# Values of both attentions as one product by seven block products, in a float32 gated mix of two attentions

## The chip, the cores and the metric

The kernel runs on one core of a Trainium2 chip. The metric is the device time of one execution in microseconds (us), the median of several. A core has TensorE (PE, with its weight loads PEld), VectorE (DVE), ScalarE (ACT), GpSimd (POOL) and SyncE (SP, which here issues nearly all DMAs). Each engine works through its own list of instructions strictly in order; an instruction that waits for another engine or for a DMA holds up all that stand behind it on the same engine.

## The reference, cut to what matters

```python
x = A_x                                       # 1 x 2048 x 512, float32
g = sigmoid((x * gate_w).sum(-1))
# A: 32 heads of 16, softmax over all 2048 keys
q, k, v = split(x @ A_wqkv)
a = softmax(q k^T / 4) v  -> (2048 x 512) @ A_wo
# B: 4 segments of 512 with a causal mask inside a segment and a memory M, z across them
q, k, v = x @ B_wq, x @ B_wk, x @ B_wv
for s in range(4):
    a_dot = softmax(q_s k_s^T / 4 + mask) v_s
    a_mem = (phi(q_s) M) / (phi(q_s) z + 1e-6)
    o_s   = sigmoid(beta) * a_mem + (1 - sigmoid(beta)) * a_dot
    M, z  = M + phi(k_s)^T v_s, z + sum phi(k_s)
b = o @ B_wo
out = g * a + (1 - g) * b
```

So x is multiplied by six 512x512 weights: A's q, k, v and B's q, k, v. This change is about the two v.

## The kernel before, in words

**Precision.** TensorE's fast float32 format (fp32r) keeps fewer bits, so every operand is split into a high part (a cast on ACT) and a low part (a subtraction of the cast from the original, on DVE or POOL), and every product is three matmuls: low by high, high by low, high by high (`PARTS`). One 512x512x512 product thus costs 4 (rows) x 4 (depth) x 3 = 48 matmuls of 128x512.

**Two stages.** The first 280 us prepare: the projections of x (here called X, in four chunks of 512 tokens), their stores to DRAM in the layout that the heads want, B's memory, the gate. The second stage, from the first score (line 1045) on, is the attention proper with scores, exponentials and products with v. The change lies in the first stage alone. 96 row maxima are wanted there ahead of the scores: `some_max` computes four of them at a time, with four matmuls (line 242) and four reductions on DVE (line 275), and `loads(n)` brings the q and k rows that they use back from DRAM.

**Slots.** The first stage is written as a sequence of slots. `slot` issues 12 matmuls of 128x512, in four places of three, and behind each place it calls the functions that were posted for that slot and place: copies out of PSUM, casts, subtractions, stores, loads. A posted function only puts instructions at the ends of the engines' lists; the slot number thus sets the order on every engine, and the semaphores set the time. Before the change there are 86 slots:

- slots 0 to 7: values of A for chunks 0 and 1 (`v_tiles`, four slots each);
- slots 8 to 15: queries of A for chunks 0 and 1 (`qk_tile`, one slot for each 128 rows of the output);
- slots 16 to 22: keys of A for chunks 0 and 1 as one 512x1024 product. `pair_tiles` cuts it in blocks, 2 by 2 in the weights and 2 by 2 in X, and makes it out of seven block products instead of eight, by Winograd's scheme: block sums S of X (`s_sums`, `s_split`) and T of the weights (`t_sum`, `t_split`), seven products in PSUM, and sums of these in `out_tile` and `sums`, on DVE;
- slots 23 to 30 values of A for chunks 2 and 3, slots 31 to 37 their keys in the same seven products;
- slots 38 to 85: for each chunk four slots of B's queries, four of B's values, four of B's keys. Behind B's queries and keys come phi, the products of the memory (`mem_q`, `mem_k`).

The groups of first maxima start in slot s0+12 = 50 and stand in 8 of each 12 slots; `loads(0)` is posted for slot s0+6 = 44. In the code `s0` is 38.

**Engines in the first stage.** ACT makes the copies out of PSUM (line 432, 537) and the casts (433, 479, 575); DVE the low parts of the results (440, 485), most low parts of operands (576), the sums out of PSUM (476, 500, 502); POOL the block sums of the weights (663), those of X for chunks 2 and 3 (646 to 649), some low parts (576), `tensor_scalar_min` for phi (437) and small DMAs, among them eight that spread `beta` over partitions (line 740, slot 8). PSUM has eight banks of 128x512: two of `pr_ps`, two of `me_ps`, four of `me_sm`. A matmul into a bank waits until the bank's last reader is through. SP's DMAs use eight semaphores in turn, so an issue waits for the landing of the eighth before it. Results' high and low parts pass through three buffers each (`q1`, `q2`): a cast into one waits until the store from it three results earlier has landed.

Of the kernel before, what the change touches and what calls it, by code (L numbers as in the profile page):

```python
# [10 lines left out]
F32 = mybir.dt.float32  # L11
# [8 lines left out]
D = 512  # L20
H = 32
DH = 16
CH = 512
# [24 lines left out]
def gated_mix(ctx, tc, x, xT, wqkv, a_wo, b_wq, b_wk, b_wv, b_wo, beta, gate_w, out):  # L48
# [284 lines left out]
    with ExitStack() as p0:  # L333
        wp = p0.enter_context(tc.tile_pool(name="wp", bufs=1))
        raws = p0.enter_context(tc.tile_pool(name="raws", bufs=3))
        xp = p0.enter_context(tc.tile_pool(name="xp", bufs=1))
        vp = p0.enter_context(tc.tile_pool(name="vp", bufs=1))
# [11 lines left out]
        ones = wk1.tile([2, CH], F32, name="ones")  # L349
        nc.vector.memset(ones, 1.0)  # L350

# [8 lines left out]
        def slot(products=()):  # L362

            for place in range(4):
                for ps, l, r, start, stop in products[3 * place:3 * place + 3]:
                    nc.tensor.matmul(ps, l, r, start=start, stop=stop)  # L366
                for f in posted.pop((now[0], place), []):
                    f()
            now[0] += 1
# [8 lines left out]


        def halves(pool, tag, src, load_slot, split_slot, tiles=None, queue=nc.sync, eng=nc.vector):  # L380

            hold = {}

            def load(i):
                t = tiles[i] and tiles[i]() if tiles else None
                if t is None:
                    t = raws.tile([128, 2, D], F32, tag="raw", name="raw")
                if isinstance(t, list):
                    for k in range(2):
                        queue.dma_start(t[k], src[256 * i + 128 * k:256 * i + 128 * k + 128])  # L390
                        hold["raw", 2 * i + k] = t[k]
                else:
                    queue.dma_start(t, src[256 * i:256 * i + 256].rearrange("(k p) d -> p k d", p=128))
                    for k in range(2):
                        hold["raw", 2 * i + k] = t[:, k]

            def split(k):
                if k == 0:
                    hold[0] = pool.tile([128, KT, D], F32R, tag=tag + "h", name=tag + "h")
                    hold[1] = pool.tile([128, KT, D], F32R, tag=tag + "l", name=tag + "l")  # L400
                w = hold["raw", k]
                nc.scalar.copy(hold[0][:, k], w)
                eng.tensor_sub(hold[1][:, k], w, hold[0][:, k].bitcast(F32))
            if load_slot is None:
                load(0)
                load(1)
            else:
                ls = load_slot if isinstance(load_slot, tuple) else (load_slot,) * 2
                post_at(ls[0], 2, lambda: load(0))
                post_at(ls[1], 3, lambda: load(1))  # L410
            for k in range(KT):
                post_at(split_slot + k // 2, 2 * (k % 2), lambda k=k: split(k))
            return hold
# [4 lines left out]
        def qk_tile(w, xc, o, dst, then=None, side="B", bank=None):  # L418

            ps = bank() if bank else pr_ps.tile([128, CH], F32, tag="pr", name="pr")  # L420
            whole(ps, lambda a, k: w[a][:, k, o * 128:(o + 1) * 128], lambda b, k: xc[b][:, k, :])
# [17 lines left out]
            def e1():  # L439
                nc.vector.tensor_sub(q2, full, q1.bitcast(F32))  # L440
# [14 lines left out]
        def pair_tiles(w, ts, xs, ss, cs, dst, eng_):  # L455

            steps, odd = [], [0]
            for g in range(2):
                col = slice(128 * g, 128 * g + 128)

                def quarter(i, j, col=col):
                    return lambda a, k: w[a][:, 2 * i + k, 256 * j:256 * j + 256][:, col]
# [946 lines left out]
```

## Time and profile before

| what | value |
|---|---|
| time, three runs | 1745.16, 1745.83, 1746.33 us (median 1745.83) |
| span of the profiled execution, first to last instruction | 1744.5 us, 1.3 us under the median |
| busy: PE, DVE, ACT, POOL | 1738.4, 1597.1, 1436.5, 736.5 us |
| granted TensorE clock | 1.000 |
| first score matmul (line 1045) | 279.9 us |

The page gives shares of the whole span; the first stage is one sixth of it, so its own busy times are to be read from windows of the trace. Times in the trace are from the span's start. Where a group of instructions has a mean in ns, that is the mean duration of one; a row of the timeline gives start, duration (of all, where several are joined with x2) and, in brackets, how long the engine sat idle before and for whom.

### The profile page before, as it was taken

What the parts mean: (1) busy time and instruction counts of PE and PEld (TensorE: products, weight loads), DVE (VectorE), ACT (ScalarE), POOL (GpSimd) and SP (SyncE); (2) the same over time, 40 slices, a digit from 0 to 9 for tenths busy, and PEclk for the clock granted to TensorE, in tenths of its full rate; (3) what the DMA queues carried; (4) which work ended last, traced back from release to release, by engine and by line L of the source; (5) the groups of instructions that cost most, each with busy time, mean ns of one, the idle gap of its engine ahead of it and who ended that gap; (6) DMA issues with size and microseconds to landing.
All of it is one profiled execution on the core that took longest, in us unless ns stands there. A gap on an engine that the chain in (4) does not pass through costs nothing.

```text
span 1744.5 us, 41555 instructions
## 1 busy us (share of the span) xinstructions
PE 1738.4 (100%) x15205; PEld 885.8 (51%) x15205; DVE 1597.1 (92%) x3327; ACT 1436.5 (82%) x2763; POOL 736.5 (42%) x992
## 2 busy tenths in 40 slices
PE   9999999999999999999999999999999999999999
PEld 7887775444444444444444444444444444444445
DVE  7757788999999999999999999999999999999931
ACT  6545557888888898888888888888888888888884
POOL 3543233234352427352534353535344353535443
PEclk9999999999999999999999999999999999999999
DMA  6787567335453446454545454444445444545542
GB/s 209 251 291 227 194 226 215 110 102 145 127 153 105 138 119 183 131 137 136 143 122 157 122 143 130 134 145 122 149 130 148 130 127 124 148 115 147 149 154 63
DMA packets 149387, 261.62 MB, mean 150 GB/s; under 512 B 39064, under 2 KB 61624, under 8 KB 148672
## 3 DMA queue, kind: packets, MB, share of 16 engines
q1 hardware_dynamic: 146640, 254.42, 49.2%
q0 software_dynamic: 2400, 4.29, 0.9%
q8 instruction: 121, 1.98, 0.5%
q14 instruction: 82, 0.67, 0.1%
q10 hardware_dynamic: 144, 0.26, 0.1%
HBM read 174.39 MB, written 83.25 MB: 148 GB/s over the span
## 4 chain that ended last, share of the span: by engine, by line
PE 99%; ACT 0%; DMA 0%; DVE 0%; issue 0%; SPq 0%; ACTq 0%; DVEq 0%
PE ops L155 40%; PE st L1045 28%; PE sm L242 14%; PE pr L366 9%; PE pair L366 4%; PE sm L155 2%; PE mt_ps L232 0%; PE tps L831 0%; PE sm L1045 0%; DMA vs<-wqkv 0%; PE mps L845 0%; PE num L804 0%; PE den L808 0%; ACT p L1068 0%; DVE pm L275 0%
## 5 line engine op out<-in xcount | busy, mean ns | idle before, releaser
L1068 ACT ACTIVATE p<-st 128x512 f32<-128x512 f32 x2261 | 1190.7, 600 | 147.6 <-PE sm L242 98.6
L275 DVE TENSOR_REDUCE pm<-sm 128x1 f32<-128x512 f32 x2048 | 1276.5, 683 | 9.7 <-PE sm L242 8.7
L242 PE MATMUL sm<-kA,qA 48*128 48x512 f32 x2048 | 662.5, 424 | 0.1
L1045 PE MATMUL st<-qA,kA 50*128 50x512 f32 x2014 | 656.2, 432 | 0.0
L155 PE MATMUL ops<-p,vA 128*17 128x256 f32 (+3 forms) x6360 | 553.0, 445 | 0.0
L1045 PEld LDWEIGHTS st<-qA,kA 50*128 50x128 f32 x2014 | 326.8, 185 | 423.4 <-ACT p L1068 378.9
L242 PEld LDWEIGHTS sm<-kA,qA 48*128 48x128 f32 x2048 | 337.8, 185 | 11.3 <-DVE ph L449 3.9
L1169 POOL TENSOR_TENSOR rcp<-rec,minus 128x32 f32<-128x32 f32 x43 | 234.8, 5461 | 78.3 <-DMA rec<-dend 73.5
L290 DVE CUSTOM_DVE_ANT_0 rest<-sm,mask 128x128 f32<-128x128 f32 (+3 forms) x512 | 246.8, 482 | 0.8 <-PE sm L242 0.7
L155 PEld LDWEIGHTS ops<-p,vA 128*17 128x17 f32 x6360 | 129.2, 96 | 216.1 <-issue 185.0
L1049 POOL TENSOR_SCALAR_AFFINE_SELECT p<-p 128x512 f32<-128x512 f32 x128 | 79.4, 637 | 270.4 <-ACT p L1068 265.7
L242 PE MATMUL sm<-kB,qB 48*128 48x128 f32 (+3 forms) x512 | 166.1, 384 | 0.0
L1045 PE MATMUL st<-qB,kB 50*128 50x512 f32 (+1 forms) x495 | 105.4, 330 | 0.3 <-ACT mt L235 0.3
L1045 PEld LDWEIGHTS st<-qB,kB 50*128 50x128 f32 x495 | 68.6, 186 | 62.2 <-ACT p L1068 50.5
L155 PE MATMUL ops<-p,vB 128*17 128x128 f32 (+3 forms) x1504 | 88.3, 350 | 0.0
L242 PEld LDWEIGHTS sm<-kB,qB 48*128 48x128 f32 x512 | 79.9, 184 | 0.0
L214 POOL TENSOR_TENSOR dm<-pm 128x32 f32<-128x32 f32 x32 | 7.9, 247 | 169.9 <-DVE pm L275 169.9
L437 POOL TENSOR_SCALAR mn<-full 128x512 f32<-128x512 f32 x24 | 36.7, 1527 | 75.6 <-ACT full L432 75.6
L223 POOL CAST ms<-pm 128x16 fp32r<-128x16 f32 x32 | 6.3, 196 | 127.5 <-DVE pm L290 127.5
L1185 POOL TENSOR_TENSOR v<-v,inv 128x512 f32<-128x512 f32 x31 | 39.8, 1283 | 28.1 <-DMA inv<-rdA 21.9
L155 PEld LDWEIGHTS ops<-p,vB 128*17 128x17 f32 x1504 | 33.8, 96 | 30.1 <-issue 26.1
L440 DVE TENSOR_TENSOR q<-full,q 128x512 fp32r<-128x512 f32 x40 | 29.2, 731 | 18.6 <-ACT q L433 15.8
(319 smaller groups left out, 1690.9 us busy)
## 6 DMA issues: line engine op xcount, KB each, us to landing
kA<-kdA SPq DMA_DIRECT2D x256, 128.0 KB
vA<-vdA SPq DMA_DIRECT2D x31, 544.0 KB
kA<-kdA SPq DMA_DIRECT2D x256, 64.0 KB
qB<-qdB SPq DMA_DIRECT2D x192, 64.0 KB
kB<-kdB SPq DMA_DIRECT2D x192, 64.0 KB
kdA<-q SPq DMA_DIRECT2D x32, 256.0 KB
qdB<-q SPq DMA_DIRECT2D x32, 256.0 KB
qA<-qdA SPq DMA_DIRECT2D x64, 128.0 KB
```

What stands on the lines that cost most here:

```text
L155: behind[0] = nc.tensor.matmul(*args, **kw)
L242: nc.tensor.matmul(ps[:, n0:n0 + n], rows(qt[u][:, :, s * 128:(s + 1) * 128], h, 48), rows(k[:, :, k0:k0 + n], h, 48), start=True, stop=True)
L275: nc.vector.tensor_reduce(pm[:, h, s, kc:kc + 1], ps, axis=AX.X, op=ALU.max, negate=True)
L290: nc.vector.tensor_tensor_reduce(out=tri["rest"][:, 0:w], in0=ps[:, n0:n0 + w], in1=tri["mask"][:, CH - w:], scale=-1.0, scalar=3.0e38, op ...
L366: nc.tensor.matmul(ps, l, r, start=start, stop=stop)
L437: nc.gpsimd.tensor_scalar_min(ph["mn"], full, 0.0)
L440: nc.vector.tensor_sub(q2, full, q1.bitcast(F32))
L1045: nc.tensor.matmul(ps[:, n0:n0 + CH - q0], rows(k[:, :, b * 128:(b + 1) * 128], h, 50), rows(q[:, :, q0:], h, 50), start=True, stop=True)
L1049: nc.gpsimd.affine_select(out=x, in_=x, pattern=[[0, 4], [1, 128]], base=0, channel_multiplier=-1, compare_op=ALU.is_ge, fill=0.0)
L1068: nc.scalar.activation(p[:, h], ps, AF.Exp, scale=SCALE)
L1169: eng.tensor_tensor(r, rec, minus, op=ALU.pow)
L1185: eng.tensor_mul(k["v"], k["v"], k["inv"])
```

## The change

**One product for both values.** The weights of A's and B's values stand side by side as one 512x1024 matrix W = (A's wv, B's wv). For a pair of chunks, X (1024 tokens) by W is again a 2 by 2 by 2 block product, and `v_pair` makes it of seven products of block sums instead of eight, for chunks 0, 1 and for chunks 2, 3. A block product of v_pair is two slots (24 matmuls). B's values are thus ready for all chunks ahead of the B slots; they are stored to `vdB` in DRAM and brought back by `load_vB` for the memory products.

**Sums in PSUM.** `k_pair` takes the place of `pair_tiles`. In both the products p1, p6, p5, p3 add into one bank X and p7, p4 add into one bank Y (p2 has Y before them), so that only three sums are left to DVE for an output group instead of seven. In return an accumulating bank must be copied out (ACT) between two products that both add to it.

**Slots now: 82.** v_pair's p1 and p2 are slots 0 to 3; A's queries for chunks 0 and 1 slots 4 to 11 (`fill=queries`); p6, p7, p5, p3, p4 slots 12 to 21; the keys of chunks 0 and 1 slots 22 to 28, those of chunks 2 and 3 slots 29 to 35; values for chunks 2 and 3 in two halves of seven slots, 36 to 42 and 43 to 49; then, for each chunk of B, four slots of queries and four of keys, 50 to 81 (`S0 = 50`). Matmuls of 128x512 at the slots' line go from 1032 to 984.

**First maxima.** One group behind each of the slots 38 to 49, and then behind every second slot of 50 to 81 (three of these places are the memory's). `loads(0)` is posted for slot 36, `loads(16)` for slot 37.

**Moved work.** T3, T4 of the value weights and S3 of X are formed on POOL, the low parts of T1 to T4 too, the key weights' block sums and most of their low parts as well, and the low parts of the key results of p5 and p3. Weights that POOL's queue loaded are loaded by SP. Values that are sums go from DVE straight into the tile `vs` (`tensor_add` with a PSUM input). Tiles are shared otherwise (`unit4`, `pieces`); B's x chunks and weights are brought in by a new `staged`.

Core of the diff, with `...` where it is cut:

```diff
-        def pair_tiles(w, ts, xs, ss, cs, dst, eng_):
...
+        ORDER = (("p1", "11", "11"), ("p2", "12", "21"), ("p6", "S2", "T2"), ("p7", "S3", "T3"), ("p5", "S1", "T1"),
+                 ("p3", "S4", "22"), ("p4", "22", "T4"))
+        def k_pair(xo, cs):
...
+            def done(p, g):
+                if p == "p1":
+                    t["1", g] = copy_x(g, "full")
+                elif p == "p2":
+                    V.tensor_add(t["1", g], Y[g], t["1", g])
+                    out_tile(g, 0, t["1", g], g, V)
+                elif p == "p6":
+                    t["a", g] = copy_x(g, "am")
+                elif p == "p5":
+                    t["5", g] = copy_x(g, "full")
+                    V.tensor_add(t["5", g], Y[g], t["5", g])
+                    out_tile(2 + g, 1, t["5", g], g, P)
+                elif p == "p3":
+                    out_tile(2 + g, 0, copy_x(g, "full"), g, P)
+                elif p == "p4":
+                    V.tensor_add(t["a", g], Y[g], t["a", g])
+                    out_tile(g, 1, t["a", g], g, V)
...
+        def v_pair(xo, cs, bs, fill=None, tags=("full", "full", "am", "am")):
...
+            ybanks = [pr_bank, pr_bank, me_bank, me_bank] if len(bs) == 4 else [me_bank] * 2
+            for p, x, w in ORDER:
+                x, w = xo[x], vops[w]
+                if fill and p == "p6":
+                    fill()
...
+        for n, place, f in ((6, 3, lambda: t_sum("T1", *vb, V)), (7, 0, lambda: t_sum("T3", *vb, P)),
+                            (7, 1, lambda: s_sum("S1", x0, x1, V)), (7, 2, lambda: t_sum("T2", *vb, V)),
+                            (7, 3, lambda: s_sum("S3", x0, x1, P)), (8, 2, lambda: s_sum("S2", x0, x1, V)),
+                            (9, 0, lambda: t_sum("T4", *vb, P)), (9, 1, lambda: op_split(vops["T2"], vr[1][2:4], P)),
...
-        for n in range(5):
-            post_at(s0 + 6 + 3 * n, 2, lambda n=n: loads(16 * n))
-        for n in range(12, 64):
-            if n in (18, 30, 42):
-                post_at(s0 + n, 3, lambda c=n // 12: mem_q(c))
-            elif n // 12 > 2 or n % 12 < 8:
-                post_at(s0 + n, 3, some_max)
+        for n in range(36, S0):
+            if n == 36:
+                post_at(n, 0, lambda: loads(0))
+                post_at(n + 1, 0, lambda: loads(16))
+            elif n > 37:
+                post_at(n, 3, some_max)
+        v_pair(xo1, (2, 3), range(2), tags=("full", "full"))
+        v_pair(xo1, (2, 3), range(2, 4), tags=("full", "full"))
```

**POOL's list ahead of product p6.** Before, from its first memsets on; `ph`, `am` and `raw` hold raw weights or X, the `kB` tiles and `wql` are low parts, `gh` is the gate of the heads:

```order
14 L740 DMA gh<-beta 16x4x1 x8
15 L663 TENSOR_TENSOR ph<-ph 128x256 x2
16 L663 TENSOR_TENSOR ph<-am,ph 128x256 x2
17 L663 TENSOR_TENSOR am<-am,ph 128x256 x2
18 L663 TENSOR_TENSOR am<-am 128x256 x2
19 L576 TENSOR_TENSOR kB_200<-ph,tk 128x256 x2
20 L576 TENSOR_TENSOR kB_201<-ph,tk 128x256 x2
21 L576 TENSOR_TENSOR kB_200<-am,tk 128x256 x2
22 L576 TENSOR_TENSOR kB_201<-am,tk 128x256 x2
```

After the change, same place; the first row is T3's sums, the second S3's, the fourth T4's, and the fifth the low parts of T2, which p6 multiplies:

```order
13 L605 TENSOR_TENSOR u_245<-u_245 128x512 x2
14 L594 TENSOR_TENSOR u_247<-u_246,u_247 128x512 x2
15 L756 DMA gh<-beta 16x4x1 x8
16 L605 TENSOR_TENSOR u_244<-u_244,u_245 128x512 x2
17 L403 TENSOR_TENSOR u_255<-u_245,u_255 128x512 x2
18 L403 TENSOR_TENSOR u_256<-u_245,u_256 128x512 x2
19 L403 TENSOR_TENSOR u_626<-u_244,u_626 128x512 x2
20 L403 TENSOR_TENSOR u_647<-u_244,u_647 128x512 x2
```

The sums are 128x512 instead of 128x256; four of them stand ahead of the eight DMAs, and six more sums and eight DMAs stand ahead of T2's low parts.

**DVE's list at the same time.** After the change, between the first query results and product p6; rows 19, 21, 25, 27, 29 are low parts of query results, row 23 is T1's sums, for which POOL's row 13 waits, and row 26 T2's:

```order
19 L434 TENSOR_TENSOR q_402<-full,q_401 128x512
20 L403 TENSOR_TENSOR u_254<-u_245,u_254 128x512
21 L434 TENSOR_TENSOR q_423<-full,q_422 128x512
22 L403 TENSOR_TENSOR u_254<-u_245,u_254 128x512
23 L605 TENSOR_TENSOR u_244<-u_245,u_244 128x512 x2
24 L594 TENSOR_TENSOR u_247<-u_247 128x512 x2
25 L434 TENSOR_TENSOR q_450<-full,q_449 128x512
26 L605 TENSOR_TENSOR u_245<-u_245,u_244 128x512 x2
27 L434 TENSOR_TENSOR q_487<-full,q_486 128x512
28 L594 TENSOR_TENSOR u_246<-u_247,u_246 128x512 x2
29 L434 TENSOR_TENSOR q_518<-full,q_517 128x512
30 L403 TENSOR_TENSOR u_258<-u_246,u_258 128x512 x2
```

All of these have both inputs in SBUF; the same stretch before holds the sums S of X and the low parts of X and of the key weights instead.

**SP's list at the first loads for the maxima.** Before, the loads of `loads(0)` (line 177) stand behind the stores of B's queries of chunk 0 (line 429):

```order
76 L429 DMA qdB_107<-q_1338 128x512
77 L429 DMA qdB_107<-q_1339 128x512
78 L429 DMA qdB_115<-q_1365 128x512
79 L429 DMA qdB_115<-q_1366 128x512
80 L177 DMA qA_1421<-qdA_59 16x1024
81 L177 DMA qA_1421<-qdA_59 32x1024
82 L177 DMA qA_1421<-qdA_59 16x1024
83 L177 DMA qA_1421<-qdA_59 32x1024
84 L177 DMA kA_192<-kdA_60 32x1024
```

After, they stand directly behind the last stores of the keys of chunks 2 and 3:

```order
62 L465 DMA kdA_66<-q_1194 128x512
63 L465 DMA kdA_66<-q_1195 128x512
64 L465 DMA kdA_74<-q_1205 128x512
65 L177 DMA qA_1220<-qdA_59 16x1024
66 L177 DMA qA_1220<-qdA_59 32x1024
67 L177 DMA qA_1220<-qdA_59 16x1024
68 L177 DMA qA_1220<-qdA_59 32x1024
69 L177 DMA kA_192<-kdA_60 32x1024
```

The maxima that use these rows came six slots behind the loads' place in the program (44 to 50), and now come two slots behind it (36 to the end of 38).

**ACT's list at the keys of chunks 2 and 3.** Before, at their end: casts of finished sums (line 479), each of which waits for DVE, and one copy of a p1 (line 492):

```order
84 L479 CAST q_1142<-full 128x512
85 L479 CAST q_1160<-full 128x512
86 L492 COPY p_1170<-pair 128x512
87 L479 CAST q_1187<-full 128x512
88 L479 CAST q_1223<-full 128x512
89 L479 CAST q_1240<-full 128x512
90 L479 CAST q_1252<-full 128x512
```

After, at the same keys (slots 32 to 36), copies that free an accumulating bank (line 479) alternate with casts of results (line 468):

```order
87 L479 COPY full<-pair 128x512 x3
88 L468 CAST q_1138<-full 128x512
89 L479 COPY full<-pair 128x512
90 L468 CAST q_1151<-full 128x512
91 L479 COPY full<-pair 128x512
92 L468 CAST q_1167<-full 128x512
93 L479 COPY full<-pair 128x512
94 L468 CAST q_1179<-full 128x512
95 L468 CAST q_1194<-full 128x512
96 L468 CAST q_1205<-full 128x512
```

Copies that PE waits for now stand behind casts that wait for stores.

More of the change, by code (lines that the diff above doesn't have):

```diff
@@ L377, in post_at @@
             posted.setdefault((n, place), []).append(f)
[L380 to L410, printed above, removed]
@@ L439, in e1 @@
             def e1():
-                nc.vector.tensor_sub(q2, full, q1.bitcast(F32))
+                low.tensor_sub(q2, full, q1.bitcast(F32))
                 store(1, q2)
@@ L571, in load_half @@
[L571 to L598 removed]
+        sm_bank = lambda: me_sm.tile([128, CH], F32, tag="sm", name="pair")
```

556 lines of the change are left out of this document (285 added, 271 removed).

## Prediction, made before the change was run

> **What bounds the kernel now.** I read the page first, then PE's waits in the first stage, then windows of that stage.
>
> ```profile
> span 1744.5 us, 41555 instructions
> PE 1738.4 (100%) x15205; PEld 885.8 (51%) x15205; DVE 1597.1 (92%) x3327; ACT 1436.5 (82%) x2763; POOL 736.5 (42%) x992
> PE 99%; ACT 0%; DMA 0%; DVE 0%; issue 0%; SPq 0%; ACTq 0%; DVEq 0%
> ```
>
> The chain that ended last is PE's own list, 99% of it. DVE's 92% is mostly earned in the second stage; what it is in the first is a matter for windows. PE's waits in the first 320 us:
>
> ```profile
> PE idle L348 <- POOL heads L81: 1.4, 1, 1.4
> PE pair L366 <- DVE xah L626: 0.3, 1, 0.3
> ```
>
> No product behind the very first one waits for anything that is worth a row. Windows (columns: PE, PEld, DVE, ACT, POOL busy, then the granted clock, DMA share, GB/s):
>
> ```profile
> 20.00:140.00 120.00, 120.00 (x531) 99.13 (x530) 80.23 (x112) 67.03 (x125) 60.91 (x76) 1.00 0.78 261
> 40.00:60.00 20.00, 20.00 (x90) 16.48 (x89) 11.88 (x16) 11.61 (x23) 10.04 (x11) 1.00 0.95 318
> 60.00:80.00 20.00, 20.00 (x90) 16.56 (x89) 17.72 (x22) 8.24 (x15) 16.15 (x12) 1.00 0.49 180
> 140.00:160.00 20.00, 19.90 (x156) 14.61 (x156) 18.71 (x36) 11.72 (x22) 11.42 (x10) 1.00 0.59 191
> ```
>
> PE is busy all the time; the helpers have room in the mean, but 17.7 and 18.7 of 20 us on DVE in single stretches, and DMA is near its limit in others. So time can only come from fewer matmuls, and it stays won only if the block sums, splits, copies and loads that make up for them are never late.
>
> **The matmuls removed.** Two products of one slot each, in a stretch of the timeline:
>
> ```profile
> 11.84 0.39 PE L366 MATMUL pair<-wvh,xah 128*128 128x512 f32 x1
> 14.56 0.61 PE L366 MATMUL pair<-wvh,xah 128*128 128x512 f32 x2
> ```
>
> The rows are the first matmuls of two slots that follow each other: 2.72 us for 12, 0.227 each. The long window agrees: 120 us by some 529 (531 less those that straddle its edges) is 0.227. The change leaves 984 of 1032, so 48 x 0.227 = **-10.9 us**, exactly four slots. The maxima, the memory products and the second stage keep their instructions; I take them at nothing, covered by PE's own list as now. What is left is to count where PE will wait.
>
> **First wait: slot 4.** The four PSUM banks of p2 end nearly together, and DVE adds them to p1's copies one after another:
>
> ```profile
> 60.11 0.69 DVE L476 TENSOR_TENSOR full<-pair,u 128x512 f32<-128x512 f32 x1
> 60.72 0.68 DVE L502 TENSOR_TENSOR u<-pair,u 128x512 f32<-128x512 f32 x1
> 61.32 0.68 DVE L476 TENSOR_TENSOR full<-pair,u 128x512 f32<-128x512 f32 x1
> ```
>
> Sums with a PSUM input come every 0.60 us and take 0.68. The first query product wants the bank that the third of them reads (`me`). Slot 3 ends at 17.44 if the first four slots run as now (14.56 + 2.72, and a wait of 0.16 as now); its first bank is whole some 0.55 earlier, so the third sum ends at 16.9 + 1.2 + 0.68 = 18.8: **+1.3 us**. Slot n then starts at 18.8 + 2.72 (n - 4).
>
> **Second wait: p6 at slot 12.** It needs the low parts of T2, and these are the last of a chain on POOL. Rows for that chain:
>
> ```profile
> 27.20 4.33 POOL L740 DMA_DIRECT2D gh<-beta  x8 [0.31 <-issue]
> 59.80 1.30 POOL L576 TENSOR_TENSOR wql<-raw,wqh 128x512 fp32r<-128x512 f32 x1
> 64.02 1.74 POOL L646 TENSOR_TENSOR ph<-raw,ph 128x512 f32<-128x512 f32 x1
> L646 POOL TENSOR_TENSOR ph<-raw,ph 128x512 f32<-128x512 f32 x2 | 3.5, 1745 | 0.0
> L648 POOL TENSOR_TENSOR raw<-ph,raw 128x512 f32<-128x512 f32 x2 | 2.9, 1456 | 0.2
> L649 POOL TENSOR_TENSOR raw<-raw 128x512 f32<-128x512 f32 x2 | 2.9, 1456 | 0.2
> L647 POOL TENSOR_TENSOR raw<-raw 128x512 f32<-128x512 f32 x2 | 2.6, 1298 | 0.2
> ```
>
> and for DVE beside it:
>
> ```profile
> 61.92 2.69 DVE L485 TENSOR_TENSOR q<-full,q 128x512 fp32r<-128x512 f32 x2
> 65.94 1.74 DVE L485 TENSOR_TENSOR q<-full,q 128x512 fp32r<-128x512 f32 x1 [0.73 <-ACT q L479]
> L440 DVE TENSOR_TENSOR q<-full,q 128x512 fp32r<-128x512 f32 x39 | 28.5, 732 | 17.2 <-ACT q L433 14.5 <-DMA qdB<-q 2.6
> L433 ACT CAST q<-full 128x512 fp32r<-128x512 f32 x39 | 24.2, 621 | 6.9 <-DMA qdA<-q 5.5 <-DMA kdA<-q 0.2
> L432 ACT COPY full<-pr 128x512 f32<-128x512 f32 x38 | 22.1, 583 | 12.4 <-PE pr L366 6.4 <-issue 3.7 <-DVE q L440 2.3
> ```
>
> A POOL sum alone takes 1.30 us, a DVE subtraction 0.73; where both engines work on two SBUF inputs at once, POOL takes up to 1.74 and DVE 1.74, while the PSUM sums of 60.1 to 62.0 kept their 0.68 with POOL at work. POOL's chain starts with T1's sums on DVE, which stand behind the second query's low part. Slot 5 ends at 18.8 + 5.4 = 24.2; copy 0.58 and cast 0.62 on ACT, low part 0.73, one weight split and the first T1 sum at 0.69 each give about 27.5. From there: four sums, the eight gate DMAs (4.2 between two rounds), two sums of T4, two low parts.
> - Undisturbed: 27.5 + 8 x 1.30 + 4.2 = 42.1.
> - All at the shared price: 27.5 + 8 x 1.74 + 4.2 = 45.6.
> - PE needs the last of them about 0.9 us into slot 12, at 41.4: waits of 0.6 and 4.2.
>
> The four groups of POOL sums above, in a stretch where DVE was 89% busy, have a mean of 1.49. In the new stretch nearly all of DVE's work has two SBUF inputs, which was not so there, so I take halfway between 1.49 and 1.74: 8 x 1.62 + 4.2 + 27.5 = 44.6, **+3.2 us** (0.6 to 4.2).
>
> The Trainium skill, "SBUF — State Buffer", section "Who interferes with whom", has the two engines share a port pair as an exclusive lock held for a whole instruction, the loser fully blocked. By that rule each POOL sum would also wait out a 0.69 us DVE operation, 1.99 in all, and p6 would wait 6.2 instead of 3.2 us. The trace agrees that such pairs slow each other and that PSUM inputs don't, but POOL loses 0.44 there and DVE 1.05.
>
> After this wait the chains of T3, T1 and T4 on POOL and of S on DVE and ACT run just ahead of slots 14 to 20, because PE has been held; if slot 12 were on time, part of the wait would come back there. I count it once. The key weights' sums and splits on POOL, behind T4's, are ready about 1.7 us ahead of slot 25: nothing.
>
> **Third wait: accumulating banks of the key products.** p5's two halves are followed by p3's on the same two banks, each 1.36 us (half a slot) later; between them ACT must copy 128x512 (0.58) behind whatever it has in its list, at most one cast (0.62): 0.2 us over, once for each pair, **+0.4** (0 to 2).
>
> **Fourth wait: the first maxima.** These are in the way of PE behind slot 38. The loads of `loads(0)` in the trace, and their landings:
>
> ```profile
> L177 SPq DMA_DIRECT2D kA<-kdA x8: 365/494/910, 129.1 to 139.6; - x8
> DMA to landing us min/median/max: 3.1/5.4/7.4
> ```
>
> The last key result's high part is cast some 3.3 us after slot 35's last matmul (copies, DVE's sums, six casts in ACT's list). Then SP issues its store and eight loads; PE's first maximum wants the last of them. With 0.49 per issue and the shortest landing, 3.3 + 0.5 + 7 x 0.49 + 3.1 = 10.3 against three slots, 8.2: 2.1 us. With 0.37 per issue it is 1.1, with the median landing 4.4. The loads before ran at a DMA share near 0.9, and in the new place less is under way, so I take **+2.1** (0 to 4.4; zero, as the depth of the queue behind slot 35 is only counted).
>
> **Maxima in twelve slots in a row.** DVE now has four reductions in each of the slots 38 to 49:
>
> ```profile
> L275 DVE TENSOR_REDUCE pm<-sm 128x1 f32<-128x512 f32 x96 | 59.6, 682 | 9.0 <-PE sm L242 8.7
> L242 PE MATMUL sm<-kA,qA 48*128 48x512 f32 x97 | 18.6, 447 | 0.1
> ```
>
> A slot with a group is 2.72 plus between 4 x 0.227 and 4 x 0.447, so 3.6 to 4.5 us of PE. DVE has four reductions (59.6 / 96 = 0.62 each in a row) and, by its list, two or three sums or splits of 0.6: 3.7 to 4.3 us. It fits, narrowly. I count nothing; if DVE shares its ports as above for half of the splits, it is 0.2 a slot, 2.4 us. In the slots 50 to 81 the values' copies and B's value weights are gone, and a group comes every 5.4 us: nothing.
>
> **Sum.** -10.9 + 1.3 + 3.2 + 0.4 + 2.1 = -3.9 us, on the profiled execution 1744.5 - 3.9 = 1740.6, on the median 1745.83 - 3.9 = **1741.9**. With the lower ends, -10.9 + 1.3 + 0.6 = -9.0 (1736.8); with the upper ends, -10.9 + 1.3 + 4.2 + 2 + 4.4 = +1.0 (1746.8).
>
> **Rivals.**
>
> *Almost all of it is hidden.* POOL's sums run at 1.30, the loads land in 3 us from a shorter queue, ACT keeps up: 1.3 to 3 us of waits and a time of 1737 to 1739, say **1738**. For it: the row of 1.30 at 59.80, with DVE on PSUM sums. Against it: the 1.74s where both engines read SBUF twice.
>
> *ACT's list becomes the bound in the key pairs (slower).* In slots 32 to 36 each copy that frees a bank stands behind a cast, and a cast waits for the landing of the store three results earlier. The trace has one such wait:
>
> ```profile
> 50.71 0.62 ACT L433 CAST q<-full 128x512 fp32r<-128x512 f32 x1 [4.67 <-DMA qdA<-q]
> ```
>
> Now a result comes every 1.36 us at the end of a pair, so three buffers allow 4.1 us from cast to landing. With a landing of 6.4 us (between the median and the longest above) and 1.0 for cast and issue, a result takes 7.4 / 3 = 2.5 us, 1.1 more than PE's half slot; five results in each of two pairs are 11 us. 1741.9 + 11 = **1753**. It decides from landings of about 4 us in that stretch, and turns the sum to slower from about 5.5. For it: DMA share 0.95 in the window of 40 to 60 us. Against it: all of ACT's line 433 casts together waited 6.9 us before, and only two copies of a pair are really wanted by PE.
>
> *DVE bounds the twelve slots of maxima.* 2.4 us as worked out: **1744.3**.
>
> *The clock falls.* The windows show a granted clock of 1.00 throughout, but also no gap in PE. If the wait at slot 12 let it fall by half for one slot, that slot would take 2.7 us more: **1744.6**. The Trainium skill, "TensorE: Matmul & The Clock Gate", Part 1, states such a fall after about one idle window of some 3.4 us; no run here shows it.
>
> That the change doesn't take out its 48 matmuls can be ruled out by the order of PE's list.
>
> **How the numbers follow.** 0.2% is 3.5 us, about what a measurement of this kernel can tell from no change. The forecast case (1740 to 1744) gets 0.50, of which a little over half lies beyond 3.5 us; hidden waits 0.22; DVE-bound maxima 0.12; the clock 0.05; ACT's list 0.11. Faster: 0.28 + 0.22 = 0.50. Slower: 0.11 and a little of the others, 0.12. Same: 0.38. The range reaches from the lower ends, 1736.5, to a little beyond the upper ends together with one of the smaller rivals, 1748; the slower rival is left out.
>
> **What would show it.** Right: the first score some 4 us earlier than 279.9; PE waits behind DVE (`vs`) at slot 4 of 1.3 us, behind POOL's line 403 at about 41 us of 3 us, behind a DMA into `kA` or `qA` before the first row of line 242 of 2 us; POOL sums with means between 1.5 and 1.7 between 27 and 45 us. Wrong: the wait at slot 12 under 1 us, or PE waits behind ACT's line 479 of more than 2 us in all, or any new wait beyond slot 50 or in the second stage, where I count none.

## The result and the profile after

The changed kernel takes 1768.3 us (median of four runs, 1766.34 to 1769.57) against 1745.9 us beside it: ratio 1.0129, 95% interval 1.0115 to 1.0143. It is 22 us slower where the forecast was 4 us faster. The page of the changed kernel, its span, busy times and chain:

```profile
span 1766.5 us, 41587 instructions
PE 1735.9 (98%) x15157; PEld 880.9 (50%) x15157; DVE 1599.9 (91%) x3321; ACT 1445.3 (82%) x2779; POOL 770.4 (44%) x1014
PE 92%; POOL 2%; ACT 2%; issue 1%; DVE 1%; DMA 1%; SPq 0%; ACTq 0%; POOLq 0%; DVEq 0%
```

The 48 matmuls are gone (15205 to 15157), but the chain now leaves PE for 8% of the span. The first score comes at 301.3 us instead of 279.9, and the second stage is as long as before to within 0.6 us: all of the loss lies in the first stage. PE's waits there, but for one ahead of the first product that both kernels have:

```profile
PE pr L385 <- ACT full L426: 12.6, 8, 5.8
PE st L1056 <- ACT full L426: 3.2, 2, 2.3
PE pair L385 <- POOL u L403: 3.0, 2, 2.3
PE sm L242 <- DMA kA<-kdA: 2.3, 1, 2.3
PE mps L855 <- ACT pt L843: 1.8, 2, 1.3
PE pr L385 <- DVE vs L545: 1.3, 1, 1.3
PE pair L385 <- ACT full L479: 0.2, 1, 0.2
```

The four foretold waits stand there to within 0.2 us: 1.3 us for DVE's sums at slot 4 (line 545), 3.0 for POOL's low parts at slot 12 (line 403), 2.3 for the loads of the first maxima, 0.2 for ACT's line 479. What the prediction did not list is the first row and its kin: 12.6 + 3.2 + 1.8 = 17.6 us behind ACT's copies of queries and keys (line 426) and of the transposed phi (843). Of these, 14.4 us lie in B's slots, 50 to 81, and 3.2 at the first two scores (line 1056), right behind the last slot. Windows show where (PE, PEld, DVE, ACT, POOL busy, then clock, DMA share, GB/s), first two of the kernel before, then four of the changed kernel:

```profile
200.00:220.00 20.00, 20.00 (x184) 13.31 (x184) 14.52 (x26) 9.01 (x17) 3.18 (x4) 1.00 0.47 164
220.00:240.00 20.00, 20.00 (x95) 15.18 (x93) 16.05 (x30) 12.08 (x22) 7.61 (x5) 1.00 0.86 296
```

```profile
40.00:60.00 20.00, 16.82 (x60) 12.82 (x59) 13.73 (x13) 10.37 (x20) 14.26 (x12) 0.83 0.26 94
200.00:220.00 20.00, 15.79 (x131) 10.99 (x130) 15.53 (x31) 9.86 (x19) 13.51 (x9) 1.00 0.72 227
220.00:240.00 20.00, 14.20 (x90) 9.37 (x89) 6.55 (x11) 10.13 (x20) 8.30 (x10) 0.83 0.65 225
240.00:260.00 20.00, 18.22 (x204) 13.36 (x203) 18.56 (x32) 10.02 (x18) 17.34 (x15) 1.00 0.79 243
```

Over the 60 us from 200 to 260 no engine of the changed kernel is full: PE, the busiest, works for 80% of them, and between 220 and 240 us for 71%. That is the look of a chain of latencies, not of a full engine. And the mean clock is 0.83 in two of the windows.

Two mechanisms can be read in the timelines. The first is at the memory's products with the queries, slot 64. DVE, ACT, then SP of the changed kernel:

```profile
223.22 0.69 DVE L443 SCALAR_TENSOR_TENSOR ph<-full,ex 128x512 f32<-128x512 f32 x1 [3.26 <-PE den L818]
```

```profile
224.00 0.63 ACT L438 ACTIVATE ex<-mn 128x512 f32<-128x512 f32 x1 [2.53 <-DVE ph L443]
224.54 2.02 ACT L824 COPY am<-num 128x512 f32<-128x512 f32 x4
231.69 0.58 ACT L426 COPY full<-pr 128x512 f32<-128x512 f32 x1 [5.13 <-DMA numd<-am]
```

```profile
219.19 5.67 SPq L423 DMA_DIRECT2D kdB<-q  x4
224.95 1.82 SPq L784 DMA_DIRECT2D u<-x  x4
226.87 2.66 SPq L825 DMA_DIRECT2D numd<-am  x4
```

Read from the top: the key's phi needs one of four buffers, and the products of the memory (PE) still hold them all; ACT's exponential waits for that phi; the copies of the products (`am<-num`) stand behind the exponential in ACT's list; their stores stand on SP behind four loads for the gate; and as these copies sit in the two buffers each of `full` and `am`, ACT's next copy of a key out of PSUM waits until a store has landed. PE stands for 5.8 us. In the kernel before, the products came among the value slots, which need neither phi nor `full`; its ACT copies the products at 172.5 us and wants `full` again at 180.0, and no copy of it waits for a store of numd:

```profile
172.51 2.05 ACT L814 COPY am<-num 128x512 f32<-128x512 f32 x4 [4.20 <-PE num L804]
180.03 0.59 ACT L432 COPY full<-pr 128x512 f32<-128x512 f32 x1 [1.83 <-issue]
```

The second mechanism is in the slots where a low part of x for the next chunk is formed on POOL (ACT, then POOL):

```profile
206.98 0.63 ACT L438 ACTIVATE ex<-mn 128x512 f32<-128x512 f32 x1 [2.15 <-POOL mn L431]
207.98 0.62 ACT L402 CAST u<-u 128x512 fp32r<-128x512 f32 x1
```

```profile
208.68 1.67 POOL L403 TENSOR_TENSOR u<-u,u 128x512 fp32r<-128x512 f32 x1 [1.74 <-ACT u L402]
210.32 1.93 POOL L431 TENSOR_SCALAR mn<-full 128x512 f32<-128x512 f32 x1
```

ACT's exponential waits for POOL's minimum; behind it on ACT comes the cast for the split; POOL's low part waits for this cast; and behind the low part on POOL comes the next minimum. One round of this loop is a slot, 4.4 to 5.3 us from one exponential to the next, while PE's own instructions in these slots fill 3.1 to 4.3 us. The kernel before has no such loop: there DVE formed these twelve low parts (line 403, 0.69 us each; six of them in the row below, where the tile `wql` holds x), and POOL formed none of them. Moving them to POOL is a part of the change that neither the list of moved work nor the prediction names.

```profile
L403 DVE TENSOR_TENSOR wql<-raw,wqh 128x512 fp32r<-128x512 f32 x6 | 4.0, 688 | 5.5 <-ACT wqh L402
```

### The profile page after: what moved, and what is told of

The parts are those of the page before. It is cut to its first block, busy times and chain, and to the rows that moved or that the text cites. A ratio compares the mean times of both kernels' runs of the same rounds, so it can differ in the third digit from the quotient of the medians.

```text
span 1766.5 us, 41587 instructions
## 1 busy us (share of the span) xinstructions
PE 1735.9 (98%) x15157; PEld 880.9 (50%) x15157; DVE 1599.9 (91%) x3321; ACT 1445.3 (82%) x2779; POOL 770.4 (44%) x1014
## 4 chain that ended last, share of the span: by engine, by line
PE 92%; POOL 2%; ACT 2%; issue 1%; DVE 1%; DMA 1%; SPq 0%; ACTq 0%; POOLq 0%; DVEq 0%
PE ops L155 40%; PE st L1056 27%; PE sm L242 14%; PE pr L385 6%; PE pair L385 2%; PE sm L155 2%; POOL mn L431 1%; DMA numd<-am 1%; POOL u L403 0%; PE mt_ps L232 0%; ACT u L402 0%; PE sm L1056 0%; ACT full L426 0%; PE idle L346 0%; ACT pt L843 0%
## 5 line engine op out<-in xcount | busy, mean ns | idle before, releaser
L385 PE MATMUL pr<-u,u 128*128 128x512 f32 x392 | 103.4, 403 | 12.7 <-ACT full L426 12.6
L385 PEld LDWEIGHTS pr<-u,u 128*128 128x128 f32 x392 | 72.9, 191 | 33.2 <-ACT full L426 15.2
```

The lines of the kernel that those rows point to most:

```text
L385: nc.tensor.matmul(ps, l, r, start=start, stop=stop, skip_group_check=chained)
```

## The experiments

Four kernels alter the changed kernel (`own_tiles` in two respects, the others in one) and one alters the kernel before; the others stand on one another, and each says on which. Times are medians of four to eleven executions, each trace is of one. The interval of a time against the kernel before is some 2 to 3 us either way (1.5 for the two kernels with eleven executions), so where two altered kernels differ by 1 to 3 us, only the waits in their traces are read, not the times. A "gap" is the time from the start of one matmul to the start of the next, 0.23 us where PE doesn't wait; the rows above count a wait from the end of the matmul before.

**Is the lost cover the cause? From both sides.** `own_tiles`, on the changed kernel:

```diff
-                am = wk.tile([128, CH], F32, tag=("full", "am")[i % 2], name="am", bufs=2)
+                am = room[i]                        # room = unit4(2, F32), four tiles
-            t = unit4((3, 7, 2, 2)[c], F32)         # gate loads, at S0 + (2, 8, 14, 20)
+            t = unit4((3, 7, 6, 6)[c], F32)         # at S0 + (2, 8, 16, 22)
```

> The changed kernel with one thing altered: the four sums of a memory product (numd) are copied to four tiles of their own instead of the two buffers each of full and am, which the next key products need at once; to make room, the gate's loads of x for chunks 2 and 3 go to another tile and come two slots later. Theory A (cover lost): without B's value slots between queries and keys, the keys' copy out of PSUM waits for the landing of the numd stores, three times (5.1, 0.5 and 3.3 us of ACT's waits), and PE and its clock follow. Then the three waits go and the time falls by 8 to 12 us, from 1768.3 to 1756 to 1760. Rival B (ACT, POOL and DMA queues are simply overloaded in these slots): the copy then waits for the next thing, and the time falls by less than 3 us, to 1765 or more.

Measured: 1758.6 us (1757.9 to 1762.9), 9.7 less. ACT's waits for numd are gone, and PE's waits behind line 426 are down to pieces of at most 1.3 us:

```profile
PE pr L385 <- ACT full L426: 7.7, 10, 1.3
```

`gate_loads_only` has the second half of that edit and not the first.

> The changed kernel (1768.3 us) with the gate's loads of x for chunks 2 and 3 two slots later and in another tile, numd's copies where they are. If numd's buffers are the cause (theory A), only the 1.8 us by which these loads delay the numd stores go: 1765 to 1768. If the loads were the cause: 1760 or less.

Measured: 1773.7 us, 5 more, against what was expected of it. In the traces 1.7 of these lie ahead of the first score (303.0 us against 301.3); the other 3.8 lie behind it, where the clock was at half for 13.7 us in this trace and for 3.4 in the changed kernel's. The first of the three waits shrank from 5.8 to 1.4 us as the loads no longer stood ahead of the stores there, but the loads for chunk 3 now stood ahead of the second group of stores, and there ACT waited:

```profile
260.90 1.87 SPq L784 DMA_DIRECT2D u<-x  x4
262.88 2.61 SPq L825 DMA_DIRECT2D numd<-am  x4
```

```profile
268.13 0.59 ACT L426 COPY full<-pr 128x512 f32<-128x512 f32 x1 [5.57 <-DMA numd<-am]
```

So a gate load ahead of numd's stores is what makes one of these waits long, and wherever it stands, numd's hold on `full` makes PE pay for it. With own tiles that hold is gone, and the gap at that place was 0.8 us with the loads where they are here.

`before_memq_late`, on the kernel before: the memory's products among its keys.

```diff
-            if n in (18, 30, 42):
+            if n in (22, 34, 46):
                 post_at(s0 + n, 3, lambda c=n // 12: mem_q(c))
+            elif n in (18, 30):
+                continue
```

> The kernel before the change, with one thing altered: the memory's products with the queries stand four slots later, among the key slots as in the changed kernel, instead of among the value slots. Theory A (the value slots were the cover): the same waits for numd stores and for phi's buffers appear at three places, and the time rises by 6 to 12 us, from 1745.9 to 1752 to 1758. Rival B (the changed kernel's fuller queues are needed for it): under 2 us more.

Measured: 1758.9 us (1757.2 to 1759.8), 12.4 more than the kernel before. The old kernel, with all its value slots, loses by this move alone more than half of what the change lost. The same chain shows, with another weight: phi's buffers first, numd's store only 1.05 us. PE's listed waits are 5.8 us together; the rest of the 12.4 is in half clock behind them (from 191.3 to 194.7 and 249.3 to 256.1 us) and in smaller gaps.

```profile
186.00 0.63 ACT L444 ACTIVATE ex<-mn 128x512 f32<-128x512 f32 x1 [4.32 <-DVE ph L449]
190.62 0.59 ACT L432 COPY full<-pr 128x512 f32<-128x512 f32 x1 [1.05 <-DMA numd<-am]
```

**The loop between ACT and POOL.** `splits_dve` puts the low parts of x's chunks 1 to 3 on DVE (`P` to `V` in three calls of `staged`); `splits_behind` leaves them on POOL and posts them at place 2 instead of 0 of their slots.

> The changed kernel with the low parts of x's chunks 1, 2 and 3 for B formed on DVE instead of POOL. Theory C (a loop between ACT and POOL): in these slots POOL's low part stands ahead of the minimum for phi, and ACT's cast for it stands behind the exponential that waits for the minimum of the slot before, so that a slot takes 4.9 us instead of PE's 3.6. Then PE's waits between 200 and 217 us and at 253 and 257 go, 5 to 8 us in all: 1760 to 1763. Rival D (those waits come from something else, the copies or the maxima): less than 2 us.

> The changed kernel with the same splits of chunks 1, 2 and 3 left on POOL, but posted two places later in the same slots, so that they stand behind the minimum for phi in POOL's list and behind the copy out of PSUM in ACT's. Theory C (the order in the lists makes the loop): nearly the same gain as with DVE, 4 to 7 us: 1761 to 1764. Rival E (POOL has too much work, 1.3 to 1.9 us for each of two operations a slot): under 2 us, 1766 or more.

Measured: 1769.4 and 1768.5 us: no gain at all. Yet PE's waits between 200 and 217 us did go in `splits_dve`, all but 1.0 us. The gap at slot 64 then was 6.9 us instead of 6.1; the first score came at 299.4 us, 1.9 sooner than in the changed kernel, but the second stage took 3.6 us longer, as the clock at its head was at half for 13.7 us instead of 3.4:

```profile
300.00:320.00 20.00, 19.09 (x134) 9.48 (x134) 16.17 (x44) 14.08 (x27) 6.59 (x8) 0.66 0.63 180
```

As the theory had not said that, both were repeated on `own_tiles`, where numd holds nothing up.

> The kernel own_tiles (four tiles of their own for numd) with the splits of x's chunks 1 to 3 on DVE as well. Base 1758.6 us. Theory C (a loop between ACT and POOL in the slots with splits, masked in the two runs on splits by the numd waits and the clock behind them): own_tiles' waits behind ACT's copies, 7.7 us in all, fall by 5 or more: 1752 to 1754. Rival D (they come from the copies and maxima): 1757 or more.

> The kernel own_tiles with the splits left on POOL but two places later. Theory C (order in the lists): nearly as good as on DVE, 1753 to 1755. Rival E (POOL's work itself): 1757 or more.

Measured: 1753.9 (1753.6 to 1754.6) and 1755.6 us (1754.0 to 1757.2), 4.7 and 3.0 less than `own_tiles`. Waits behind line 426 fell from 7.7 to 3.5 us with DVE and to 5.3 with the other order. The loop was real, since undoing it on this base gives what theory C said. The order in the lists is at least a part of it; whether DVE is better than the other order the two times, 1.7 us apart, can't tell. On the changed kernel itself both showed nothing, as a longer wait at slot 64 and the half clock took up what was won.

**The waits that were foretold.** On `own_tiles`: the gate DMAs at slot 24 (`post_at(8, 0` to `post_at(24, 0`), and the first maxima behind slot 39 (`n > 37` to `n > 38`).

> The kernel own_tiles with the eight small gate DMAs posted for slot 24 instead of slot 8, so that POOL forms T2's low parts 4.3 us sooner. By the prediction's second term: the two waits at slot 12, 3.0 us (and 0.9 more of gaps there), go nearly all, and with them the half clock behind them, which cost 1.7 to 3.4 us: 1758.6 falls by 5 to 7 us, to 1752 to 1754. Rival (T2's low parts wait for DVE's sums and ACT's casts as well, which are as late): under 2 us.

> The kernel own_tiles with the first group of maxima behind slot 39 instead of slot 38. By the prediction's fourth term the loads have one slot more: the wait of 2.4 us goes, and the half clock behind it (1.7 us in this base): 1758.6 falls by 3 to 4 us, to 1754.6 to 1755.6. Rival (the loads are late because of the queue, and the wait moves with the maxima): under 1 us.

Measured: 1758.5 and 1757.6 us, 0.1 and 1.0 less, neither clear of noise, and not the 5 to 7 and 3 to 4 expected. In the second the wait for the loads went, but PE waited 0.8 us more behind line 426, 0.7 at the first scores, and its clock was at half for as long as before. In the first, POOL's wait went from the list, but another took its place; PE's waits in it, and DVE's list there:

```profile
PE pair L385 <- ACT kA L402: 2.3, 1, 2.3
```

```profile
28.16 3.48 DVE L594 TENSOR_TENSOR u<-u 128x512 f32<-128x512 f32 x2
37.26 3.48 DVE L594 TENSOR_TENSOR u<-u,u 128x512 f32<-128x512 f32 x2
```

DVE's sums for S1 and S2 take 1.74 us each here, while POOL works beside them, and S2's are as late as T2's low parts were. In the changed kernel S2's sums ran while POOL issued its DMAs (34.7 to 39.0 us), at 0.64 us each. `sums_dve`, on `own_tiles_splits_dve`, takes POOL out of this stretch:

```diff
-(7, 0, lambda: t_sum("T3", *vb, P))       -(7, 3, lambda: s_sum("S3", x0, x1, P))
+(7, 0, lambda: t_sum("T3", *vb, V))       +(7, 3, lambda: s_sum("S3", x0, x1, V))
-(9, 0, lambda: t_sum("T4", *vb, P))       -(9, 1, lambda: op_split(vops["T2"], vr[1][2:4], P))
+(11, 2, lambda: t_sum("T4", *vb, P))      +(9, 1, lambda: op_split(vops["T2"], vr[1][2:4], V))
```

> The kernel own_tiles_splits_dve (1753.9 us) with the block sums T3 and S3 and the low parts of T2 formed on DVE, and T4's sums on POOL two slots later, so that POOL does next to nothing while DVE makes what product p6 needs. Theory F (the shared price: DVE's operations take 1.7 us and POOL's 1.7 where both read two SBUF inputs, so that moving only the gate DMAs could not help): DVE's 21 operations at 0.6 us from 27 us end at 40, p6 starts on time, 3 to 4 us of gaps and 1.7 of half clock go: 1748.5 to 1750. Rival G (the chain of dependences through ACT's casts is too long anyway, or the wait comes back at p7 to p4 because POOL now starts late): 1752.5 or more.

Measured: 1752.0 us, 1.9 less, which the times alone don't tell from none. In the trace all waits at slot 12 are gone, and DVE's operations come every 0.60 us there: DVE alone is in time where DVE and POOL together were not. The 3 to 4 us that were expected don't arrive at the end; in this trace the clock fell at other places (0.83 between 20 and 30 us, behind a wait of 2.1 us at slot 4, and once more behind the first maxima).

Three more on `own_tiles_splits_dve` or all of it:

> The kernel own_tiles_splits_dve (1753.9 us) with the first group of maxima behind slot 39 instead of 38. With the loop in B's slots gone, what is won early should stay won: the wait of 2.3 us for the loads goes: 1751 to 1752. Rival (as with own_tiles alone, where it gave 1.0: another wait takes its place in the slots of B): 1753 or more.

> The kernel own_tiles_splits_dve (1753.9 us) with the memory's products with the queries one slot earlier (and the groups of maxima where they were, none in the freed places), ahead of the first key's phi, so that DVE needs no phi buffer that these products still hold. Gaps of 0.6, 0.8 and 0.5 us at three places go: 1752 to 1753. Rival (the same copies of ACT delay the next key product either way): 1753.5 or more.

> All of it: own tiles for numd, splits and early sums on DVE, gate DMAs at slot 24, first maxima behind slot 39, memory products one slot earlier, and the queries of chunks 0 and 1 taking the pr banks first (their sums end first at slot 4: 1.2 us). If the terms add: 1753.9 - 4.5 - 2.3 - 1.2 - 1.2 = 1744.7, within 0.1 per cent of the kernel before; if waits move on instead of going, 1748 or more.

Measured: 1752.7, 1758.4 and 1752.7 us. The maxima a slot later give 1.2 of the 2.3 us, within the noise. The memory's products a slot earlier are a loss of 4.5: PE's waits in B's slots do go (line 426: 3.5 to 0.3 us), but the first score comes 2.6 us later than in the base, with half clock behind the first maxima that the base's trace doesn't have, and the second stage is 2.0 us longer: it begins with gaps of 1.1, 0.7 and 1.3 us after 288 us, with the clock at 0.95 and 0.88. What makes this loss I did not follow up. `all_parts` loses at the same place: its second stage takes 1467.7 us, 2.8 more than that base's.

**The clock.** `clock_filled`, on `splits_dve_maxima_later`: eleven matmuls into a bank that nobody reads, posted behind slot 11.

> The kernel splits_dve_maxima_later (1752.7 us) with eleven matmuls of 128x512 (2.5 us) ahead of product p6, into a free bank that nobody reads: they run where PE waited 2.8 us for POOL. If the clock's fall is caused by the gap, it stays at 1.00 behind slot 12, and the 3.4 us of half clock there go: 1749 to 1750.5. If the fall has another cause, or the fill only lengthens PE's list: 1752.5 to 1755.

Measured: 1751.9 us, 0.8 less. Windows of the base and of this kernel:

```profile
40.00:60.00 20.00, 17.49 (x62) 13.21 (x62) 13.68 (x14) 10.86 (x20) 14.18 (x12) 0.83 0.27 95
```

```profile
40.00:60.00 20.00, 19.00 (x83) 15.09 (x82) 14.77 (x15) 11.16 (x21) 13.95 (x12) 1.00 0.27 95
```

With the gap filled the clock stays at 1.00, so the gap is what lowers it. Its price there is hidden, though: the window holds 83 matmuls instead of 62 (eleven of them the fill), and slot 15 starts 2.1 us sooner against the base; but then PE waits 1.0 us for a copy ahead of slot 19 (at 64 us), and from slot 24 to slot 57 (80 to 183 us) the distance between the two kernels is again what it was ahead of the fill, to within 0.2 us. A PE at half pace had only come later to helpers that were late anyway, as the prediction had said of slots 14 to 20. The 0.8 us at the end are not clear of noise.

**Can the parts beat the kernel before?** `best_parts` is `all_parts` with the memory's products where the changed kernel has them. The two others put the splits of x, or the minimum for phi, on the other engine.

> all_parts (1752.7 us) with the memory's products where the changed kernel has them. all_parts reached its first score at 281.8 us but then lost 3 us at the head of the second stage, as splits_dve_memq_early did, with waits that the other runs don't have. Without them: 1748 to 1750. If the parts hide each other's gains: 1751 or more.

> best_parts (1747.1 us) with the splits of x's chunks 1 to 3 back on POOL, behind the minimum for phi. If DVE's list bounds B's slots now (phi stands behind reductions, gate sums and splits), 0.6 us less of DVE in each of eleven slots give 1 to 3 us: 1744 to 1746, at or below the kernel before. If POOL's shared price or its low parts come back as the bound: 1748 or more.

> best_parts with the minimum for phi on DVE instead of POOL. If POOL's 1.5 us in the chain copy, minimum, exponential, phi bounds those slots: 1743 to 1745. If DVE's list does: 1747 to 1750.

Measured: 1747.1 us (11 runs, 1746.7 to 1748.3; ratio to the kernel before 1.0010, interval 1.0001 to 1.0018), 1750.9 and 1748.7. `best_parts` has a clock of 1.000 and reaches the first score at 279.7 us, 0.2 sooner than the kernel before, with a gap of 1.1 us behind it. Its waits of PE, then those of ACT's exponential between 165 and 282 us:

```profile
PE pr L385 <- ACT full L426: 3.2, 6, 1.0
PE tps L843 <- DVE jk L777: 1.4, 1, 1.4
PE st L1058 <- ACT dn L831: 0.7, 1, 0.7
PE pair L385 <- ACT vt L525: 0.6, 1, 0.6
PE pr L385 <- DVE vs L554: 0.6, 1, 0.6
```

```profile
ACT ex L438 <- DVE ph L443: 25.6, 12, 4.2
ACT ex L438 <- POOL mn L431: 12.2, 11, 1.3
```

21 of the 22 us are back, and the 10.9 us of matmuls saved are paid out again, 6.5 of them in these waits of at most 1.4 us and the rest in smaller gaps. Of the 6.5, 4.6 lie in B's slots, where ACT's exponential now waits mostly for DVE. Neither way of shifting work between DVE and POOL made it faster: `best_splits_behind` is slower, with a wait of 3.4 us behind line 426 at 201 us, and the 1.6 us of `best_minimum_dve` are within the noise. That speaks against DVE's list or POOL's minimum alone as the bound there; that it is the chain copy, minimum, exponential, phi, once a slot, with four reductions in between, is argued from the lists and was not shown by a run.

## Why the prediction was wrong, point by point

- **Matmuls, -10.9 us:** right. 15157 are left, at the same pitch where the clock is full.
- **Slot 4, +1.3:** measured a gap of 1.69 us instead of 0.23, 1.46 more.
- **Slot 12, +3.2:** measured 3.0 in two waits, 4.3 with the smaller gaps behind them. The groups of POOL between 20 and 45 us:

```profile
L756 POOL DMA_DIRECT2D gh<-beta x8 | 4.3, 550 | 0.0
L594 POOL TENSOR_TENSOR u<-u,u 128x512 f32<-128x512 f32 x2 | 3.4, 1734 | 0.0
L403 POOL TENSOR_TENSOR u<-u,u 128x512 fp32r<-128x512 f32 x2 | 3.4, 1713 | 0.0
L605 POOL TENSOR_TENSOR u<-u 128x512 f32<-128x512 f32 x2 | 3.4, 1700 | 25.8 <-DMA qdA<-q 25.8
L605 POOL TENSOR_TENSOR u<-u,u 128x512 f32<-128x512 f32 x2 | 3.2, 1618 | 0.0
```

  The four pairs have means of 1.62 to 1.73 us; 1.62 was taken, the shared price of 1.74 was nearer. But the term's reasoning fell short in one thing, which `own_tiles_gates_late` shows: DVE pays the shared price too, so its S2 was equally late, and undoing the POOL side alone wins nothing. That the term came so near owes something to luck: POOL's chain began 0.5 us later than reckoned and its pairs took longer, but slot 12 began 0.6 us later too (41.2 us instead of 40.6).
- **Key pairs, +0.4:** measured 0.2 and small gaps, 0.4 in all. The slower rival, ACT's list in the key pairs, didn't come about.
- **First maxima, +2.1:** measured 2.3.
- **Twelve slots of maxima, nothing:** right; slots 39 to 49 take 3.61 us each, as a slot with a group does in the kernel before, and the rival that DVE bounds them has no wait in the list. (Its 0.2 us a slot is not derived in the prediction.)
- **The clock:** a rival with 0.05, and it came true. Behind the gaps at slot 12 thirteen matmuls were issued every 0.427 us instead of 0.227, 2.6 us. The Trainium skill, "TensorE: Matmul & The Clock Gate", Part 1, says a clock gate halves the clock after about one idle window of 3.4 us, and that the window runs freely. The traces agree with the half clock and with a window that runs freely: the clock falls at 44.84, 229.16 and 304.25 us in the changed kernel, 54 and 22 times 3.41 us apart, and stays at half for 3.41 or 6.83 us; in every trace all changes of the clock lie on one such grid. They differ on what makes it fall, where the measurement decides: much less than a window of idle is enough. Three stretches on this grid of the changed kernel, then two of `own_tiles`:

```profile
41.43:44.84 3.41, 1.11 (x4) 0.48 (x3) 3.41 (x3) 2.62 (x6) 3.41 (x3) 1.00 0.35 136
44.84:51.66 6.82, 6.10 (x15) 4.77 (x15) 6.82 (x7) 2.31 (x5) 4.12 (x3) 0.50 0.10 38
119.93:123.34 3.41, 1.91 (x9) 1.25 (x7) 0.00 (x0) 2.21 (x4) 1.55 (x2) 1.00 0.97 242
```

```profile
120.39:123.80 3.41, 0.97 (x6) 0.49 (x5) 0.00 (x0) 1.62 (x3) 2.73 (x3) 1.00 0.94 251
123.80:127.21 3.41, 3.41 (x9) 2.28 (x9) 2.48 (x4) 0.00 (x0) 0.55 (x2) 0.50 0.88 209
```

  At slot 12 PE is idle (by the ends that the profile models) for 2.30 us within one window, and half clock follows. The gap before the first maxima, 2.7 and 2.8 us long in the two kernels, is cut by the end of a window in the changed kernel (1.50 us of idle before it, 0.81 behind it, and the clock stays); in `own_tiles` it lies inside one window (2.44 us), and the clock falls. In the first 325 us of all nineteen traces, 26 windows at full clock have PE idle for 1.87 us or more, and half clock followed each of them; of the twelve with 1.5 to 1.85 us it followed one. Five more falls came behind less idle time, and why stays open.
- **B's slots, "nothing":** this is the step that failed. The sentence was that in slots 50 to 81 the values' copies and weights are gone and a group of maxima comes every 5.4 us. It counted the busy time that was taken away from ACT and DVE, and did not walk the chain of one slot: copy, minimum, exponential, phi, with each engine's list in between. The value slots were also time for that chain: four slots of some 11 us for each chunk, in which PE had work and phi, `full` and numd's stores could catch up. The change saved 10.9 us of PE and, with the value slots gone from between B's queries and keys, uncovered 17.6 us of PE's waits there and at the first scores, plus half clock behind them. For the memory's products that is shown from both sides: -9.7 us with `own_tiles`, +12.4 with `before_memq_late`. The other part, the loop between ACT and POOL (-4.7 us with `own_tiles_splits_dve`), came from the low parts of x that the change moved to POOL and that the prediction's walk leaves out; how much the lost cover alone would have cost there was not tested. Of the list in the prediction, the condition "any new wait beyond slot 50" was what would show it wrong, and it did.

How the 22 us stand: -10.9 for the matmuls; +1.5, +4.3, +0.4 and +2.5 for the four foretold places with their small gaps; +2.6 for the clock at slot 12; +16.7 for the waits behind ACT up to the first score (0.9 of the 17.6 fall behind it) and some 1.4 for the clock there (seven matmuls at half pace behind slot 64). That is +18.5 against +21.4 at the first score; the rest is in many smaller gaps and was not taken apart. Without B's slots and the clock the rows sum to -2.2, not far from the forecast of -3.9; but no run had just these waits.

## What to carry to other kernels

Before taking work out of the engine that bounds, ask what latency it covered: list, for one period of the shortened loop, who waits for whom through every engine's list and every buffer that is held by a store, and compare its length with what is left for the bounding engine; busy shares don't show it. When several waits stand in a row, undoing an early one may show nothing, because a later one takes up what was won, so test it again with the later ones gone. And where DVE and POOL both read two SBUF inputs, work moved to POOL is paid for on DVE as well (here 1.74 us for an operation of 0.69).

## What was not expected of the hardware

- Sums and splits with two SBUF inputs come faster from DVE alone than from DVE and POOL together: one every 0.60 us in `sums_dve`, against two every 1.74 us in `own_tiles_gates_late`, which is 0.87 for one. Sharing such work was worth less than nothing in that stretch.
- Whether the granted clock falls to half depends not on the length of a gap alone, but on how much of it lies within one of the clock's windows of 3.41 us: with PE idle for 1.87 us or more within one it fell 26 times of 26. So the same gap before the first maxima lowered it in `own_tiles` and not in the changed kernel. Eleven matmuls into an unread bank kept it at 1.00.
